# Putting a slice's pending second product directly behind its first product on TensorE, in the first block and a half of a two-layer MLP

## The chip, the cores and the metric

The kernel runs on one core of a Trainium2 chip. The metric is the time of one execution on the device in microseconds (us), the median of several runs. Engines are named as in the profile: PE (TensorE matmul), PEld (its weight load), DVE (VectorE), ACT (ScalarE), POOL (GpSimd), SP (SyncE, which issues the DMAs).

## The reference, cut to what matters

```
a = softmax(scale * x @ state.T)          # per batch and head, 512 x 32
xread = a @ state                         # 512 x 64
a2 = softmax(scale * state @ x.T); sread = a2 @ x
rows = concat([xread, sread]) -> (8 * 544, 512)
h = rows @ w1_in;  g = max(h, 0) + alpha * min(h, 0);  rows = g @ w1_out   # 512 -> 2048 -> 512
h = rows @ w2_in;  g = h - tanh(h);                    out  = g @ w2_out
```

The result is wanted in float32. The matrices are kept as two parts each (a rounded one and what it leaves), and a product is three products of parts.

## The kernel before, in words

The rows are treated in blocks: blocks 0 to 7 are the 512 read rows of a batch, block 8 the 256 state rows. In the first layer a block is worked through in 16 slices of 128 hidden columns (`f` = 0 to 15). A slice has

- a **first product** (`emit_h`, L623) of rows and the slice's columns of `w1_in`, into the PSUM tile `ps_h`: 12 matmuls of 128x128 by 128x512 in block 0, and 6 in blocks 1 to 7, whose weights have been multiplied with the states ahead (`pw`, also kept in `wo` buffers);
- an **activation** in two halves. `act_a`: ACT makes `t` (L629), DVE overwrites `ps_h` (L630). `act_b`: ACT writes the rounded part of `g` (L634), DVE the other part (L635). `g` has two buffers, so `act_b` of slice f overwrites what slice f-2 left;
- a **second product** (`emit_o`, L651): 12 matmuls of 128x512 of `g` and `w1_out`, added up over the slices in four PSUM tiles `acc`. It is done two slices later: slice f's `g` waits in the list `pend`. With a block's (or half block's) last slice, `finish` copies the four `acc` tiles into `y` (ACT L676 takes two, DVE L678 two), and SP stores them.

The order of visits is: slices 0 to 7 of block 0, all 16 of block 1, slices 8 to 15 of block 0, then the other blocks. Below, "slice 0.3" is slice 3 of block 0 and "slice 1.1" slice 1 of block 1.

The program is written in a fixed order. Each engine takes its instructions in that order, waiting on semaphores. Other work is hung into a slice by the timetable `plan`, at five places: `early` (behind the first product, ahead of `act_a`), `gap` and `mid` (behind `act_a`), `late` and `end` (behind `act_b`). The second product of two slices ago stands behind `mid`, ahead of `act_b`:

```
ph = emit_h(blk, n, f)
...            # early
act_a(n, f, ph)
...            # gap, mid
if len(pend) == 2:
    emit_o(*pend.popleft())
pend.append((blk, n, f, act_b(n, f, ph)))
...            # late, end
```

In the stretch of this change what hangs in the timetable is: the attention steps of block 1 (PE transposes `ps_xt` L477 copied by ACT L482, scores `ps_s` L511, softmax on DVE and ACT with the exponential L528, `ps_e` L546 copied by ACT L548, `ps_r` L576 scaled by DVE into `wide` L581 to L586, `ps_w` L601); state transposes (`ps_st` L365, ACT L369 and L376, DVE L377); the projection of weights by states (`ps_p` L414, 3 matmuls in `mid` and 3 in `late`, ACT L421, DVE L422) in slices 0.5, 0.6, 1.0, 1.1, 1.4, 1.5, 1.8 and 1.9; and the conversion of the raw 64-bit weights into parts (ACT L113, L127, L171 or L173; DVE L118, L120, L123; POOL L174, L180 or L183), of which a step hangs in nearly each slice.

All PSUM tiles but `acc` (`ps_h`, `ps_p`, `ps_xt`, `ps_st`, `ps_e`, `ps_s`, `ps_r`, `ps_w` and the conversion's `ps_v`) share four buffers, each handed on when its last reader has been issued; PE then waits for that reader.

Of the kernel before, what the change touches and what calls it, by code (L numbers as in the profile page):

```python
# [35 lines left out]
def attention_and_two_mlps(ctx, tc, x, state, w1_in, w1_out, alpha, w2_in, w2_out, out):  # L36
# [7 lines left out]
    NF = DFF // P  # L44
# [50 lines left out]
    def w_in(f, part):  # L95
        return WI[f // FQ][:, part].rearrange("p c (f m) -> p c f m", f=FQ)[:, :, f % FQ, :]

    def w_out(f, part):
        return WO[f // FQ][:, part, f % FQ, :]
# [251 lines left out]
    def lead(b):  # L351
        return b if b % 2 or b == B - 1 else b - 1
# [260 lines left out]
    def emit_h(blk, n, f):  # L613
        ps = ps_a.tile([P, S], F32, tag="a", name="ps_h")
        if 0 < blk < B:
            col = slice(f % FQ * P, (f % FQ + 1) * P)
            pairs = [([PW[blk, f // FQ, g][i][:, col] for i in range(2)], X[0, blk, g]) for g in range(NG)]
        else:
            w = [WS[f][:, i] if blk else w_in(f, i) for i in range(2)]
            pairs = [([w[i][:, cc, :] for i in range(2)], X[0, blk, cc]) for cc in range(NCC)]  # L620
        for k, (w, xt) in enumerate(pairs):
            for m, (i, j) in enumerate(TERMS):
                nc.tensor.matmul(ps[:, :n], lhsT=w[i], rhs=xt[:, j, :n], start=(k == 0 and m == 0),  # L623
                                 stop=(k == len(pairs) - 1 and m == 2))
        return ps[:, :n]

    def act_a(n, f, ph):
        t = work.tile([P, S], F32, tag="t", name="t")[:, :n]
        nc.scalar.mul(t, ph, slope[:, f:f + 1])  # L629
        nc.vector.scalar_tensor_tensor(ph, ph, sign[:, f:f + 1], t, op0=ALU.mult, op1=ALU.max)  # L630

    def act_b(n, f, ph):
        g = work.tile([P, 2, S], F32R, tag="g", name="g")
        nc.scalar.mul(g[:, 0, :n], ph, sign[:, f:f + 1])  # L634
        nc.vector.scalar_tensor_tensor(g[:, 1, :n], ph, sign[:, f:f + 1], g[:, 0, :n].bitcast(F32),  # L635
                                       op0=ALU.mult, op1=ALU.subtract)
        return g
# [3 lines left out]
    def emit_o(blk, n, f, g):  # L641
        w = [w_out(f, i) for i in range(2)]
        first, last = f == 0, f == NF - 1
        if blk == 0:
            first, last = first or f == NF // 2, last or f == NF // 2 - 1
        if first:
            accs[blk] = [ps_acc.tile([P, S], F32, tag="acc", name="acc") for _ in range(NCC)]
        acc = accs[blk]
        for t in range(NCC):
            for k, (i, j) in enumerate(TERMS):  # L650
                nc.tensor.matmul(acc[t][:, :n], lhsT=w[i][:, t * P:(t + 1) * P], rhs=g[:, j, :n],  # L651
                                 start=(first and k == 0), stop=(last and k == 2))
        if last:
            finish(blk, n, acc)
# [9 lines left out]
    def finish(blk, n, acc):  # L664
        for t, a in enumerate(acc):
            if blk == 0 and half_sum:
                y = half_sum[t]
                nc.vector.tensor_tensor(y, a, y, op=ALU.add)
                stores.append((blk, t, y))
                continue  # L670
            if t < 2:
                y = work.tile([P, S], F32, tag="y", name="y")[:, :n]
            else:
                y = work.tile([P, S], F32, tag="sc" if t == 2 else "at", name="y", bufs=1)[:, :n]
            if t % 2 == 0:
                nc.scalar.copy(y, a[:, :n])  # L676
            else:
                nc.vector.tensor_copy(y, a[:, :n])  # L678
            stores.append((blk, t, y))
# [3 lines left out]
    def store():  # L683
        for blk, t, y in stores:
            nc.sync.dma_start(out=y_dram[blk][t], in_=y)
        stores.clear()
# [407 lines left out]
    with tc.manual_schedule():  # L1094
# [40 lines left out]
        for b in range(2, B):  # L1135
            for g in range(NG):
                i, f = (0, 0) if b == 2 else (b - 2, 6 + 7 * g) if b == lead(b) else (b - 2, 1 + g)
# [78 lines left out]
        pend = deque()  # L1216
        visits = [(0, f) for f in range(NF // 2)] + [(1, f) for f in range(NF)] + [(0, f) for f in range(NF // 2, NF)]
        visits += [(i, f) for i in range(2, len(seq)) for f in range(NF)]
        for i, f in visits:
            blk, n = seq[i]  # L1220
            ph = emit_h(blk, n, f)
            for z in plan.get((i, f, "early"), ()):
                z()
            act_a(n, f, ph)
            for z in plan.get((i, f, "gap"), ()):
                z()
            for z in plan.get((i, f, "mid"), ()):
                z()

            if len(pend) == 2:  # L1230
                emit_o(*pend.popleft())
            pend.append((blk, n, f, act_b(n, f, ph)))
            for z in plan.get((i, f, "late"), ()):
                z()
            for z in plan.get((i, f, "end"), ()):
                z()
            store()
# [125 lines left out]
```

## Time and profile before

| | us |
|---|---|
| time before, median of 3 runs (lowest, highest) | 1465.25 (1464.43, 1468.32) |
| the profiled execution, its own time | 1464.9 |
| its span in the trace | 1463.1 |
| PE busy | 1401.1 (96%) |
| DVE, ACT, POOL busy | 964.2, 731.0, 531.3 |
| first products with `pw`, `wi` and `wo` weights, L623: PE busy | 156.7, 53.3, 20.6 |
| second products, L651: PE busy | 405.6 |

The profile is of one execution, from which all rows below come; its time is 1.8 us over its span. A mean of a group of matmuls is longer than the step from one to the next, because matmuls overlap; the time that twelve take is read from a timeline row. In a timeline row the bracket tells how long the engine was idle before the row and which instruction ended that. PE is the busiest engine, and most of its idle time lies in the first 180 us, where the changed slices are.

### The profile page before, as it was taken

What the parts mean: (1) busy time and instruction counts of PE and PEld (TensorE: products, weight loads), DVE (VectorE), ACT (ScalarE), POOL (GpSimd) and SP (SyncE); (2) the same over time, 40 slices, a digit from 0 to 9 for tenths busy, and PEclk for the clock granted to TensorE, in tenths of its full rate; (3) what the DMA queues carried; (4) which work ended last, traced back from release to release, by engine and by line L of the source; (5) the groups of instructions that cost most, each with busy time, mean ns of one, the idle gap of its engine ahead of it and who ended that gap; (6) DMA issues with size and microseconds to landing.
All of it is one profiled execution on the core that took longest, in us unless ns stands there. A gap on an engine that the chain in (4) does not pass through costs nothing.

```text
span 1463.1 us, 22894 instructions
## 1 busy us (share of the span) xinstructions
PE 1401.1 (96%) x8188; PEld 1189.7 (81%) x8188; DVE 964.2 (66%) x1430; ACT 731.0 (50%) x1322; POOL 531.3 (36%) x414
## 2 busy tenths in 40 slices
PE   5779999999999999999999999999999999999998
PEld 2556777777777777778887888888879999999998
DVE  6888655556667677765345656466347698777774
ACT  4666544445556555655334545455345354444443
POOL 2545410000454455446001212122026576656661
PEclk9999999999999999999999999999999999999999
DMA  5446528885777776769846764553978733444421
GB/s 160 126 140 182 157 77 315 306 277 148 219 196 233 214 249 198 241 212 301 261 129 231 263 244 169 202 194 128 342 279 301 262 107 130 145 138 138 144 80 37
DMA packets 227906, 288.12 MB, mean 197 GB/s; under 512 B 57808, under 2 KB 133584, under 8 KB 226768
## 3 DMA queue, kind: packets, MB, share of 16 engines
q1 hardware_dynamic: 227792, 286.66, 61.0%
q8 instruction: 64, 1.05, 0.3%
q14 instruction: 50, 0.41, 0.1%
HBM read 166.54 MB, written 117.96 MB: 194 GB/s over the span
## 4 chain that ended last, share of the span: by engine, by line
PE 58%; DVE 7%; DMA 7%; ACT 3%; issue 2%; POOL 2%; SPq 1%; ACTq 0%; DVEq 0%; POOLq 0%
PE ps_m L1033 20%; PE ps_m L843 17%; PE acc L651 11%; PE ps_h L623 6%; DMA gt<-g 1%; DMA wp<-wc 1%; DVE ps_h L630 1%; DVE g L635 1%; PE ps_p L414 1%; DMA c_raw<-in_moe_w_in 1%; PE ps_m L917 1%; ACT g L634 1%; DMA g<-ts 1%; DVE c_m L123 1%; DMA c_raw<-in_moe_w_out 1%
## 5 line engine op out<-in xcount | busy, mean ns | idle before, releaser
L651 PE MATMUL acc<-g,wo 128*128 128x512 f32 (+1 forms) x1728 | 405.6, 384 | 3.0 <-ACT g L634 1.1
L651 PEld LDWEIGHTS acc<-g,wo 128*128 128x128 f32 x1728 | 311.2, 190 | 75.2 <-issue 6.5
L1033 PE MATMUL ps_m<-wp,s 128*128 128x256 f32 x2856 | 343.2, 283 | 0.8 <-ACT e L1016 0.8
L1033 PEld LDWEIGHTS ps_m<-wp,s 128*128 128x128 f32 x2856 | 343.0, 192 | 1.1 <-ACT e L1016 1.0
L843 PE MATMUL ps_m<-x,ch 128*128 128x512 f32 x1344 | 306.5, 390 | 3.1 <-ACT c L849 2.4
L843 PEld LDWEIGHTS ps_m<-x,ch 128*128 128x128 f32 x1344 | 251.8, 188 | 57.4 <-ACT c L849 3.7
L978 DVE TENSOR_TENSOR s<-gt,s 128x512 fp32r<-128x512 f32 (+1 forms) x216 | 213.5, 1039 | 45.6 <-ACT s L994 44.6
L635 DVE SCALAR_TENSOR_TENSOR g<-ps_h,sign,g 128x512 fp32r<-128x512 f32 (+1 forms) x144 | 103.6, 720 | 167.0 <-ACT g L634 166.9
L634 ACT ACTIVATE g<-ps_h,sign 128x512 fp32r<-128x512 f32 (+1 forms) x144 | 95.5, 663 | 181.8 <-PE acc L651 130.8
L994 ACT CAST s<-gt 128x512 fp32r<-128x512 f32 (+1 forms) x216 | 120.0, 596 | 82.5 <-PE ps_m L1033 38.4
L623 PE MATMUL ps_h<-x,pw 128*128 128x512 f32 x600 | 156.7, 396 | 3.0 <-DMA pw<-pw 1.6
L630 DVE SCALAR_TENSOR_TENSOR ps_h<-ps_h,sign,t 128x512 f32<-128x512 f32 (+1 forms) x144 | 104.6, 726 | 66.0 <-ACT t L629 65.2
L623 PEld LDWEIGHTS ps_h<-x,pw 128*128 128x128 f32 x600 | 109.7, 188 | 28.6 <-DMA pw<-pw 2.0
L244 POOL TENSOR_TENSOR c_q<-c_m,c_q 128x512 int32<-128x512 int32 x32 | 41.3, 1291 | 241.0 <-DVE c_m L123 222.6
L856 POOL TENSOR_TENSOR t<-c,t 128x512 f32<-128x512 f32 x32 | 44.9, 1402 | 231.0 <-ACT t L853 226.1
L629 ACT ACTIVATE t<-ps_h,slope 128x512 f32<-128x512 f32 (+1 forms) x144 | 95.8, 665 | 54.0 <-PE ps_h L623 53.4
L865 DVE TENSOR_TENSOR c<-ps_m,c 128x512 f32<-128x512 f32 x96 | 65.8, 690 | 83.8 <-PE ps_m L843 71.7
L853 ACT ACTIVATE t<-c 128x512 f32<-128x512 f32 x96 | 60.6, 633 | 85.3 <-DVE c L865 73.8
L271 POOL TENSOR_TENSOR c_o<-c_q,c_o 128x512 fp32r<-128x512 f32 (+1 forms) x48 | 55.8, 1163 | 95.1 <-ACT c_o L269 95.1
L960 POOL TENSOR_TENSOR s<-gt,gt 128x512 f32<-128x512 f32 (+1 forms) x36 | 52.0, 1452 | 87.0 <-DMA gt<-g 86.9
L849 ACT COPY c<-ps_m 128x512 f32<-128x512 f32 x96 | 56.0, 586 | 51.4 <-PE ps_m L843 48.4
L174 POOL TENSOR_TENSOR cq<-cm,cq 128x512 int32<-128x512 int32 x32 | 42.0, 1312 | 105.2 <-DVE cm L123 81.6
(145 smaller groups left out, 1646.8 us busy)
## 6 DMA issues: line engine op xcount, KB each, us to landing
g<-t SPq DMA_DIRECT2D x128, 256.0 KB, 2.3
gt<-g SPq DMA_DIRECT2D x64, 512.0 KB, 5.0
wc<-c_o SPq DMA_DIRECT2D x112, 256.0 KB, 4.0
ch<-wc SPq DMA_DIRECT2D x56, 512.0 KB, 6.8
pw<-pw SPq DMA_DIRECT2D x96, 256.0 KB, 5.4
wp<-wc SPq DMA_DIRECT2D x28, 512.0 KB, 7.0
xr<-in_x SPq DMA_DIRECT2D x64, 128.0 KB, 3.0
raw<-in_moe_w_in SPq DMA_DIRECT2D x16, 512.0 KB, 3.9
```

Source lines behind the costliest of these rows:

```text
L623: nc.tensor.matmul(ps[:, :n], lhsT=w[i], rhs=xt[:, j, :n], start=(k == 0 and m == 0), stop=(k == len(pairs) - 1 and m == 2))
L629: nc.scalar.mul(t, ph, slope[:, f:f + 1])
L630: nc.vector.scalar_tensor_tensor(ph, ph, sign[:, f:f + 1], t, op0=ALU.mult, op1=ALU.max)
L634: nc.scalar.mul(g[:, 0, :n], ph, sign[:, f:f + 1])
L635: nc.vector.scalar_tensor_tensor(g[:, 1, :n], ph, sign[:, f:f + 1], g[:, 0, :n].bitcast(F32), op0=ALU.mult, op1=ALU.subtract)
L651: nc.tensor.matmul(acc[t][:, :n], lhsT=w[i][:, t * P:(t + 1) * P], rhs=g[:, j, :n], start=(first and k == 0), stop=(last and k == 2))
L843: nc.tensor.matmul(b, lhsT=w[p][:, cc], rhs=XT[key, i][cc][:, q], start=(i not in GOES_ON and cc == k == 0), stop=(cc == 1 and k == 2), sk ...
L853: nc.scalar.activation(t, h, AF.Tanh)
L865: nc.vector.tensor_tensor(h, ps[j, i], h, op=ALU.add)
L978: nc.vector.tensor_tensor(made[k - 1][:, 1], src, made[k - 1][:, 0].bitcast(F32), op=ALU.subtract)
L994: nc.scalar.copy(made[k][:, 0], source(blk, i, jj))
L1033: nc.tensor.matmul(dst[:, t * HW:(t + 1) * HW], lhsT=s[:, p, r, t * P:(t + 1) * P], rhs=w[:, q], start=first, stop=(jj == NJ // 2 - 1 and ...
```

## The change

In the first half of block 0 and in block 1 the second product that stands in the list is written directly behind the slice's first product, ahead of `early`. Nothing is added or taken away.

```
--- before.py
+++ after.py
             ph = emit_h(blk, n, f)
+            ahead = len(pend) == 2 and (i == 1 or i == 0 and f < NF // 2)
+            if ahead:
+                emit_o(*pend.popleft())
             for z in plan.get((i, f, "early"), ()):
                 z()
             act_a(n, f, ph)
...
-            if len(pend) == 2:
+            if len(pend) == 2 and not ahead:
                 emit_o(*pend.popleft())
             pend.append((blk, n, f, act_b(n, f, ph)))
```

`pend` holds two entries from slice 0.2 on, so 22 second products move: those written in slices 0.2 to 0.7 and 1.0 to 1.15. `finish` of block 0's first half belongs to the second product written in slice 1.1 and moves with it.

On PE in slice 0.2, the end of the first product and what follows (the difference; `g` is slice 0.0's, `sm` the masked states, `xr` the block's rows; a number behind a name is a running count of buffers):

```order
 L623 MATMUL ps_h<-x_0_3_378,wi_343 128x512 x3
+L651 MATMUL acc<-g,wo_394 128x512 x12
 L365 MATMUL ps_st<-ident,sm 128x128 x2
-L576 MATMUL ps_r<-xr_218,e2t 32x64 x16
-L651 MATMUL acc<-g,wo_394 128x512 x12
-L576 MATMUL ps_r<-xr_218,e2t 32x64 x16
+L576 MATMUL ps_r<-xr_218,e2t 32x64 x32
```

The twelve matmuls of the second product have come past the state transposes and the first `ps_r`.

On PE in slice 1.1, a slice with projections, before:

```order
L623 MATMUL ps_h<-x_1_0_897,wo_904 128x512 x3
L623 MATMUL ps_h<-x_1_1_1103,wo_904 128x512 x3
L414 MATMUL ps_p<-wi_573,snp 128x512 x3
L651 MATMUL acc<-g,wo_756 128x512 x12
L414 MATMUL ps_p<-wi_573,snp 128x512 x3
```

and of the change:

```order
L623 MATMUL ps_h<-x_1_0_909,wo_916 128x512 x3
L623 MATMUL ps_h<-x_1_1_1115,wo_916 128x512 x3
L651 MATMUL acc<-g,wo_756 128x512 x12
L414 MATMUL ps_p<-wi_589,snp 128x512 x6
L623 MATMUL ps_h<-x_1_0_909,wo_916 128x512 x3
```

The two projections, which stood around the second product, now stand together behind it and directly ahead of the next first product.

On ACT in slice 1.1, before (`y<-acc` are the copies of `finish`, `t` and `g` the slice's own activation, `wo` the rounded part of a projection, `cm` a step of the conversion):

```order
L629 ACTIVATE t<-ps_h,slope 128x512
L113 ACTIVATE cm<-raw_1148 128x512
L421 CAST wo_904<-ps_p 128x512
L676 COPY y<-acc 128x512 x2
L634 ACTIVATE g<-ps_h,sign 128x512
```

and of the change:

```order
L676 COPY y<-acc 128x512 x2
L629 ACTIVATE t<-ps_h,slope 128x512
L113 ACTIVATE cm<-raw_1148 128x512
L421 CAST wo_916<-ps_p 128x512
L634 ACTIVATE g<-ps_h,sign 128x512
```

The two copies of `finish` have come ahead of the slice's `t`; on DVE the other two stand ahead of L630 in the same way.

## Rows read from the trace of the kernel before

**Rows 1.** Stretches: us, busy of PE, PEld, DVE, ACT, POOL, PE clock, DMA share, GB/s.

```profile
45.30:110.95 65.65, 50.61 (x323) 36.35 (x324) 52.90 (x95) 38.16 (x74) 30.64 (x24) 0.95 0.43 123
110.95:180.64 69.69, 65.58 (x269) 49.76 (x270) 52.24 (x88) 45.32 (x80) 33.73 (x26) 0.95 0.64 178
180.64:260.00 79.36, 78.61 (x412) 63.24 (x411) 45.50 (x85) 35.30 (x62) 3.83 (x3) 1.00 0.55 190
260.00:300.00 40.00, 37.17 (x170) 28.39 (x172) 23.71 (x43) 18.60 (x36) 0.00 (x0) 1.00 0.96 319
...
76.89:88.64 11.75, 10.22 (x67) 7.55 (x67) 11.13 (x21) 8.10 (x16) 4.98 (x5) 0.85 0.29 94
...
110.95:121.43 10.48, 9.36 (x25) 6.06 (x26) 8.01 (x16) 6.11 (x11) 5.53 (x4) 0.67 0.42 125
```

**Rows 2.** Waits, 45 to 181 us: us in total, times, longest.

```profile
ACT g L634 <- PE acc L651: 25.0, 12, 4.0
...
PE ps_h L623 <- DVE g L635: 4.4, 5, 1.2
```

**Rows 3.** Timeline of slice 0.2: start, us, engine, instruction, idle before it.

```profile
49.73 0.69 PE L365 MATMUL ps_st<-ident,sm 128*128 128x128 f32 x2
50.38 0.70 ACT L629 ACTIVATE t<-ps_h,slope 128x512 f32<-128x512 f32 x1
52.20 3.06 PE L651 MATMUL acc<-g,wo 128*128 128x512 f32 x12
52.95 1.29 POOL L174 TENSOR_TENSOR cq<-cm,cq 128x512 int32<-128x512 int32 x1 [0.26 <-DVE cm L123]
53.30 0.96 DVE L584 TENSOR_SCALAR ri<-par,s 128x2 f32<-128x2 f32 x1
54.37 0.29 DVE L586 TENSOR_TENSOR wide<-ps_r,ri 128x128 f32<-128x128 f32 x1
55.77 3.02 PE L623 MATMUL ps_h<-x,wi 128*128 128x512 f32 x12
57.05 0.23 DVE L584 TENSOR_SCALAR ri<-par,s 128x2 f32<-128x2 f32 x1
```

**Rows 4.** Timeline of slices 0.3 to 0.7, ACT and PE.

```profile
65.54 0.69 ACT L634 ACTIVATE g<-ps_h,sign 128x512 fp32r<-128x512 f32 x1 [3.56 <-PE acc L651]
66.44 3.02 PE L623 MATMUL ps_h<-x,wi 128*128 128x512 f32 x12
76.89 4.60 PE L623 MATMUL ps_h<-x,wi 128*128 128x512 f32 x12 [2.17 <-DVE snp L377]
88.64 3.02 PE L623 MATMUL ps_h<-x,wi 128*128 128x512 f32 x12 [1.20 <-DVE g L635]
98.80 0.69 ACT L634 ACTIVATE g<-ps_h,sign 128x512 fp32r<-128x512 f32 x1 [3.95 <-PE acc L651]
100.33 3.02 PE L623 MATMUL ps_h<-x,wi 128*128 128x512 f32 x12 [0.89 <-DVE g L635]
```

**Rows 5.** Timeline of slice 1.1, PE, ACT and DVE.

```profile
121.43 1.63 PE L623 MATMUL ps_h<-x,wo 128*128 128x512 f32 x6 [0.76 <-DVE g L635]
122.90 0.84 PE L414 MATMUL ps_p<-wi,snp 128*128 128x512 f32 x3
123.10 0.69 ACT L629 ACTIVATE t<-ps_h,slope 128x512 f32<-128x512 f32 x1 [0.84 <-PE ps_h L623]
123.58 2.88 PE L651 MATMUL acc<-g,wo 128*128 128x512 f32 x12
124.23 0.58 ACT L421 CAST wo<-ps_p 128x512 fp32r<-128x512 f32 x1
125.81 0.68 DVE L422 TENSOR_TENSOR wo<-ps_p,wo 128x512 fp32r<-128x512 f32 x1
125.81 0.59 ACT L676 COPY y<-acc 128x512 f32<-128x512 f32 x1 [0.51 <-PE acc L651]
126.98 1.52 PE L623 MATMUL ps_h<-x,wo 128*128 128x512 f32 x6
```

## The prediction

> **What bounds the kernel now.** I read the page first: PE is busy nearly throughout, so time can only be won where PE idles or runs slowly. The view of stretches [rows 1] says where that is. From slice 0.2's first product to block 1's, 45.30 to 110.95 us, PE is busy 50.61 of 65.65 us: 15.0 us idle. To slice 1.12, at 180.64, it is busy 65.58 of 69.69: 4.1 idle. In the next 79.36 us it idles 0.75 us. In the two changed stretches the granted clock is 0.95, elsewhere here 1.00; by slices the loss sits in few of them (0.85 in 0.5, 0.67 in 1.0). So some 19 us of idle time, and a few more of half clock, are all that this change can touch.
>
> Then the view of waits [rows 2]. The wait that the change aims at is there: ACT's first write of `g` waits for the second product of two slices ago 12 times, 25.0 us in all, up to 4.0. It has to, since that product reads the buffer that `g` overwrites. But PE, which is the bound, waits for what follows from it (DVE's half of `g`) only 5 times, 4.4 us. What PE mostly waits for in these slices is the rest of a ring: PE side work, ACT, DVE, a PSUM buffer, the next first product. That ring is asked slice by slice below.
>
> **The change part by part.** No instruction is added or removed on any engine, and SP's and POOL's order is the same; 22 second products move. In seven of them (1.2, 1.3, 1.6, 1.7, 1.12 to 1.14) PE has nothing between first and second product, so nothing moves. In the other 15, three things happen. ACT's write of `g` no longer waits for the second product. All PE side work of `early`, `gap` and `mid` starts one second product later, 2.9 us. And `finish` of block 0's half comes ahead of slice 1.1's activation. I follow how late the next first product is against before.
>
> *Slice 0.2, 1.5 us late.* The state transpose stands in `early`, and ACT's copies of it stand ahead of `t`. Now it comes 2.9 us later: `t` starts at 50.38 + 2.9 = 53.3 [rows 3]. From the start of `t` to the end of `wide` it took 54.66 - 50.38 = 4.3 us; DVE had first to finish a conversion step, which is done by then, so I take 4.0. The next first product needs the PSUM buffer that `wide` frees: 57.3 instead of 55.77. Before, PE was in the second product (52.20 to 55.26) while that chain ran, and it is idle during it now.
>
> In this chain DVE's tiny `ri` took 0.96 us at 53.30 and 0.23 at 57.05. The first stands behind POOL's add, which ends at 52.95 + 1.29 = 54.24, and `ri` ends at 54.26 [rows 3]. [...] The 4.0 above keeps it, by the row.
>
> *Slices 0.3 and 0.4, -0.5 and +0.35.* In 0.3 the transposes `ps_xt` come later and push `t` in the same way, but the wait of 3.56 us ahead of `g` [rows 4] is gone, and what stood behind the second product (`ps_s`, next first product) no longer does: 10.2 us instead of 55.77 to 66.44, 10.67. DVE's work behind it stays about 1.35 late. In 0.4 ACT waits for the softmax anyway while PE does the second product: DVE's 1.35 becomes the next first product's.
>
> *Slices 0.5 and 0.6, -0.65 and -1.0.* These are where the change does what it can. The first products of 0.6 and 0.7 waited 1.20 and 0.89 us for DVE's half of `g` [rows 4]. That of 0.6 now gets the buffer of the first `ps_p`, whose reader stands one DVE operation ahead (0.65). In 0.6 `t` is pushed by 3.0 but the wait of 3.95 ahead of `g` goes (1.0). Lateness at 0.7's first product: -0.3.
>
> *Slices 0.7 and 1.0, +0.85 and 0.* The second projection of 0.6 needs the buffer that DVE's reading of the first one frees. That now follows behind the pushed `t`, so DVE's next work, the softmax, starts some 0.5 late, and it runs without a gap to the first product of 1.0: +0.85 against -0.3. In 1.0 the second product and a projection change places in the half clock [rows 1]: the same 15 matmuls, the same time.
>
> *Slice 1.1, +2.1.* The second copy of `finish` cannot start before the third `acc` tile is done, 125.81 - 123.58 = 2.23 us after the second product starts [rows 5]. That product now starts 1.5 us after the first, so the copy starts at 3.7 and `t`, now behind it, at 4.25 us, instead of 123.10 - 121.43 = 1.67. DVE's reading of the projection ended 126.49 - 123.10 = 3.4 us after the start of `t`; now at 7.65. The next first product needs that buffer: 7.7 us after this one instead of 126.98 - 121.43 = 5.55. Before, the second product covered this.
>
> *Projection slices 1.4, 1.5, 1.8, 1.9, and 1.10, 1.11: +0.5 together.* Now both projections stand directly ahead of the next first product, which needs the first one's buffer: 0.84 on PE, 0.58 on ACT, 0.68 on DVE and the hand-overs are 2.2 us, of which the second projection covers 1.5 [rows 5]. That is 0.7 idle a slice, about what PE idled in them before for `g` (part of the 4.4). I take +0.2, -0.4, 0 and +0.4, and +0.3 for the copy of `ps_xt` ahead of `t` in 1.10 and 1.11.
>
> *Sum:* 1.5 - 0.5 + 0.35 - 0.65 - 1.0 + 0.85 + 2.1 + 0.5 = +3.2 us at slice 1.12. From there PE is busy 99% up to 260 us, and the order is as before, so the lateness is carried to the end. Only between 260 and 300, with 2.8 us of PE idle [rows 1], could some be absorbed; the transfers there follow work that is late too, and I take nothing off. Against the profiled execution's own 1464.9 (its span is 1463.1) this gives 1468.1; that execution lies 0.35 under the median, so beside the median it is 1468.45. I predict 1468.3, 0.2% more, within the 0.3% (4.4 us) that a measurement of this kernel can tell from no change.
>
> Bounds of what no row shows. The gains cannot be more than the 4.4 us of PE waiting for `g`, unless the ring as a whole turns faster: then at most the 15.0 us. The losses are 0 to 1.5 in 0.2 (0 if PE's next product finds another buffer), 0 to 2.6 in 1.1 (the push of `t`), and 0 to 0.7 in each of the other eight, 5.6.
>
> **The rivals.** *Slower: half clock behind a longer gap.* [...] My 0.2 leaves PE with little but small transposes for nearly 4 us ahead of 0.3's first product. If the clock drops there, 0.3 costs 1.6 more, and all later steps hang on it: 3.2 + 1.6 = 4.8, 1469.9; once more in 1.1, where PE would idle 1.9 us, 1471.5. It decides from 1.2 us on, since that passes 4.4. [...] Against: the gap of 1.20 ahead of 0.6 was followed by 3.02. [...]
>
> *Faster: the 25.0 us of ACT's waiting were the ring.* Freed, ACT and DVE would run ahead with conversions and softmax, and a third of the 15.0 us would close: 1465 - 5 = 1460. For it: the wait of 3.95 us in 0.6 ends 1.5 us before the next first product [rows 4]. Against: only 4.4 us of them reach PE, and in slices with an `early` step ACT now waits for the same 2.9 us one operation sooner, ahead of `t`.
>
> *Nothing: the losses are covered.* The lateness is given back by the idle time up to 300 us, or 0.2 and 1.1 find other buffers: 0 to +1, 1465.5. For it: PE idles 2.8 us there. Against: its cause is late as well.
>
> That the second products do not move can be left out: the order of instructions shows it.
>
> **How the numbers follow.** Forecast, +1 to +4.4 us: 0.45. Covered: 0.12. Slower rival, with what of my losses exceeds their size: 0.33. Faster rival: 0.10. So slower by over 0.3% 0.33, within 0.3% 0.57, faster 0.10. The range takes in the slower rival with both drops and some error on top, 1473.5, and goes down to 1462, leaving most of the faster one out; the forecast's own range is 1466 to 1469.7.
>
> **What would show it.** In the profile after: ACT's `g` waits for `acc` only in the seven unmoved slices and in block 0's second half, under 10 us; ACT's `t` or the copies ahead of it wait instead. The first product of 0.3 comes near 57.3, of 0.7 near 100.0, of 1.2 near 129.7, of 1.12 near 184. The clock of 0.3 (1.00 or not) tells the slower rival. I am wrong if the first product of 1.0 comes much before 110.95, if 1.1 lasts under 6.5 us, or if what is lost by 1.12 is not there at 420 us.

## The result: 0.5% slower

The changed kernel takes 1472.91 us (median of 5 runs, 1471.34 to 1476.58) against 1465.53 for the kernel before in the same comparison (5 runs, 1464.43 to 1468.32). The ratio is 1.0051, 95% interval 1.0034 to 1.0069: 7.4 us slower, more than the 0.3% that can be told from no change. That lies inside the range of the prediction, but its forecast, a loss too small to be told from no change, did not come. What came is the slower rival. The profiled execution took 1476.58 us (span 1474.8), the slowest of the five.

The lengths of the slices, from one first product to the next, in the two profiled executions:

| slice | before | after | difference | forecast |
|---|---|---|---|---|
| 0.2 | 10.47 | 11.81 | +1.34 | +1.5 |
| 0.3 | 10.67 | 12.97 | +2.30 | -0.5 |
| 0.4 | 10.45 | 11.85 | +1.40 | +0.35 |
| 0.5 | 11.75 | 11.64 | -0.11 | -0.65 |
| 0.6 | 11.69 | 10.67 | -1.02 | -1.0 |
| 0.7 | 10.62 | 11.57 | +0.95 | +0.85 |
| 1.0 | 10.48 | 9.85 | -0.63 | 0 |
| 1.1 | 5.55 | 7.76 | +2.21 | +2.1 |
| 1.2 | 4.08 | 5.83 | +1.75 | 0 |
| 1.3 to 1.11 | 49.58 | 50.48 | +0.90 | +0.5 |

In sum 9.1 us at slice 1.12 where 3.2 were forecast. Four terms are right within 0.2; 0.3, 0.4 and 1.2 miss by 2.8, 1.05 and 1.75, all upward.

### The profile page after: what moved, and what is told of

It is laid out like the page before. It is cut to its first block, busy times and chain, and to the rows that moved or that the text cites. A ratio compares the mean times of both kernels' runs of the same rounds, so it can differ in the third digit from the quotient of the medians.

```text
span 1474.8 us, 22891 instructions
## 1 busy us (share of the span) xinstructions
PE 1408.8 (96%) x8188; PEld 1196.4 (81%) x8188; DVE 965.6 (65%) x1430; ACT 730.2 (50%) x1322; POOL 534.3 (36%) x414
## 3 DMA queue, kind: packets, MB, share of 16 engines
q8 instruction: 64, 1.05, 0.3%
## 4 chain that ended last, share of the span: by engine, by line
PE 55%; DMA 8%; DVE 7%; ACT 3%; issue 2%; POOL 2%; SPq 1%; ACTq 0%; DVEq 0%; POOLq 0%
PE ps_m L1033 20%; PE ps_m L843 17%; PE acc L651 10%; PE ps_h L623 5%; DMA gt<-g 1%; PE ps_m L917 1%; DVE ps_h L630 1%; DMA wp<-wc 1%; DVE g L635 1%; DMA c_raw<-in_moe_w_in 1%; ACT g L634 1%; PE ps_p L414 1%; DMA pw<-pw 1%; DVE c_m L123 1%; DVE c_m L120 1%
## 5 line engine op out<-in xcount | busy, mean ns | idle before, releaser
L651 PEld LDWEIGHTS acc<-g,wo 128*128 128x128 f32 x1728 | 314.8, 191 | 74.6 <-issue 5.0
L630 DVE SCALAR_TENSOR_TENSOR ps_h<-ps_h,sign,t 128x512 f32<-128x512 f32 (+1 forms) x144 | 104.5, 726 | 77.4 <-ACT t L629 76.9
```

## The profile after

The stretches, of the same slices as in [rows 1] (us, busy of PE, PEld, DVE, ACT and POOL, PE clock, DMA share, GB/s):

```profile
44.57:115.08 70.51, 55.01 (x323) 40.86 (x324) 53.31 (x95) 37.93 (x74) 30.59 (x24) 0.85 0.39 114
115.08:189.00 73.92, 67.18 (x270) 50.97 (x270) 52.62 (x89) 45.11 (x81) 33.74 (x26) 0.94 0.61 168
189.00:268.36 79.36, 78.61 (x412) 63.31 (x413) 45.30 (x85) 34.81 (x61) 3.83 (x3) 1.00 0.55 190
268.36:308.36 40.00, 37.22 (x174) 28.41 (x176) 23.69 (x43) 17.93 (x36) 0.00 (x0) 1.00 0.96 320
```

The first stretch is 4.86 us longer, yet PE idles 15.50 us in it where it idled 15.04: the same matmuls are just busy for 4.4 us more, and the clock is 0.85 instead of 0.95. In the third stretch PE's busy time is the same to 0.01 us as before: nothing is given back.

The wait that the change aimed at, 45 to 190 us (us in all, times, longest):

```profile
DVE ps_h L630 <- ACT t L629: 16.3, 11, 5.3
...
ACT g L634 <- PE acc L651: 5.4, 3, 3.1
...
PE ps_h L623 <- DVE wo L422: 4.0, 4, 2.0
...
PE ps_h L623 <- DVE g L635: 1.0, 3, 0.3
```

Against [rows 2], ACT's waits for the second product fall from 25.0 us to 5.4, and PE's for DVE's half of `g` from 4.4 to 1.0. So the change does what it says, but other waits grow: DVE waits 16.3 us for a later `t`, where it waited 7.4 before, and PE 4.0 us for DVE's reading of a projection (`wo`).

PE in 0.2, and the first products of 0.3 to 0.5 (start, us, instruction, idle before it and what ended it):

```profile
49.02 2.90 PE L651 MATMUL acc<-g,wo 128*128 128x512 f32 x12
51.76 0.38 PE L365 MATMUL ps_st<-ident,sm 128*128 128x128 f32 x2
52.88 0.65 PE L576 MATMUL ps_r<-xr,e2t 128*32 128x64 f32 x32 [0.74 <-DVE snp L377]
54.62 0.65 PE L576 MATMUL ps_r<-xr,e2t 128*32 128x64 f32 x32 [1.08 <-ACT snp L376]
56.38 5.49 PE L623 MATMUL ps_h<-x,wi 128*128 128x512 f32 x12 [1.10 <-DVE wide L586]
...
68.08 0.33 PE L601 MATMUL ps_w<-ident,wide 128*128 128x128 f32 x1 [1.64 <-DVE cm L123]
...
69.35 4.61 PE L623 MATMUL ps_h<-x,wi 128*128 128x512 f32 x12
...
81.20 5.43 PE L623 MATMUL ps_h<-x,wi 128*128 128x512 f32 x12 [2.90 <-DVE snp L377]
```

Three stretches of the same execution, the small steps of 0.2, all of 0.3 and all of 0.4 (columns as above):

```profile
51.76:56.38 4.62, 1.69 (x68) 1.16 (x66) 3.31 (x9) 4.31 (x11) 1.99 (x3) 0.93 0.34 110
56.38:69.35 12.97, 11.09 (x38) 7.91 (x38) 7.08 (x15) 4.87 (x9) 4.44 (x4) 0.76 0.20 64
69.35:81.20 11.85, 8.21 (x33) 6.33 (x31) 9.21 (x17) 5.94 (x14) 5.74 (x6) 0.79 0.35 102
```

In [rows 3] the second product stood between the small steps and covered the chain to `wide`. Now PE is busy 1.69 of 4.62 us ahead of 0.3, and then 12 matmuls that took 3.02 us [rows 3] take 5.49: the granted clock is 0.50 through them, where it was 1.00 through the same twelve before. 0.50 is called the lower level below, 1.00 the upper. The lower one comes again in 0.4 (first product 4.61 instead of 3.02, its mean clock 0.63) after 1.64 us of idle and a few small matmuls, and lasts longer in 0.5 (5.43 instead of 4.60, mean clock 0.52 instead of 0.63) after 2.90.

In 0.2 the rest is as forecast: POOL's add still stands ahead of DVE's tiny `ri`, which ends with it at 55.9 (0.96 us in [rows 3], 0.81 here):

```profile
54.62 1.28 POOL L174 TENSOR_TENSOR cq<-cm,cq 128x512 int32<-128x512 int32 x1 [2.63 <-ACT snp L376]
...
54.74 0.14 DVE L581 TENSOR_SCALAR s<-s 128x1 f32<-128x1 f32 x1
...
55.12 0.81 DVE L584 TENSOR_SCALAR ri<-par,s 128x2 f32<-128x2 f32 x1
```

The prediction's 4.0 us for this chain kept the 0.96 by the row, and the long `ri` came again. DVE's `s` ran its 0.14 us inside the same add, while `ri` ended only with it. In the kernel before, the nine `ri` that start outside a POOL step took 0.23 us each; the seven that start inside one took up to 1.17, and each ended 0.02 to 0.04 us behind that step. Why `ri` was held and `s` was not, no run here shows.

Slices 1.1 and 1.2 of after, ACT, DVE and PE:

```profile
124.93 1.65 PE L623 MATMUL ps_h<-x,wo 128*128 128x512 f32 x6 [0.33 <-DVE g L635]
126.42 2.90 PE L651 MATMUL acc<-g,wo 128*128 128x512 f32 x12
128.68 0.59 ACT L676 COPY y<-acc 128x512 f32<-128x512 f32 x1 [0.77 <-PE acc L651]
129.16 0.69 ACT L629 ACTIVATE t<-ps_h,slope 128x512 f32<-128x512 f32 x1
131.96 0.68 DVE L422 TENSOR_TENSOR wo<-ps_p,wo 128x512 fp32r<-128x512 f32 x1
132.69 1.66 PE L623 MATMUL ps_h<-x,wo 128*128 128x512 f32 x6 [2.00 <-DVE wo L422]
134.18 4.50 PE L651 MATMUL acc<-g,wo 128*128 128x512 f32 x12
```

`t` starts 4.23 us after the first product (forecast 4.25; 1.67 in [rows 5]), DVE's reading ends 7.71 us after it (7.65), the next first product comes at 7.76 (7.7). Behind the 2.00 us of idle, the second product of 1.2 takes 4.50 us, at a mean clock of 0.62, where others take 2.88.

## The experiments

**Theory.** Two losses add up: late steps, as in the prediction's sum (some 3.5 us), and TensorE's lower clock level where the moved second product leaves PE idle (0.3, 0.4, 1.2; some 5.5 us). **Rivals:** the late steps alone, the level being chance; the level being there but covered by other waits; only the copies ahead of `t`, or only TensorE's order, costing.

Each kernel was compared with the kernel before on the same chip; "time" is the ratio less one, times 1466 us, with its interval. "Late" is the time from 0.2's first product to that of 1.0, 1.1 or 1.12 in its profiled execution, less that in the profile of [rows 1 to 5].

| kernel | late at 1.0 | at 1.1 | at 1.12 | time |
|---|---|---|---|---|
| before_again | 1.5 | 2.1 | 2.2 | 0 (itself) |
| changed | 4.9 | 4.2 | 9.1 | +7.4 (5.0 to 10.1) |
| only_half0 | 4.0 | 3.3 | 3.6 | +1.9 (0.4 to 3.5) |
| only_block1 | 1.3 | 1.7 | 4.7 | +4.0 (2.3 to 5.6) |
| busy_02_03 | 1.2 | 0.5 | 5.0 | +4.3 (2.5 to 5.9) |
| after_busy | 0.7 | -0.9 | 3.7 | +10.8 (8.4 to 13.3) |
| before_busy | 1.5 | 1.4 | 1.4 | 0.0 (-2.1 to 1.9) |
| not_02 | 0.5 | -0.1 | 2.9 | +1.2 (0.0 to 2.5) |
| not_11 | 3.9 | 3.4 | 4.0 | +1.6 (0.3 to 3.1) |
| t_first | 0.7 | 0.4 | 3.5 | 0.0 (-1.8 to 1.6) |
| proj_later | 3.9 | 3.6 | 6.7 | +6.0 (4.0 to 7.9) |
| only_05_06 | 0.9 | 1.3 | 1.7 | -0.7 (-2.1 to 0.6) |
| best | -1.3 | -1.1 | -1.3 | -1.9 (-3.7 to 0.0) |

**A control.** The kernel before, unchanged, profiled once more.

> The kernel before once more, unchanged, for a second profile of it: three kernels whose 0.3 is that of before had its second product at the lower clock level (4.3 us instead of 3.0), the one profiled execution of before had not. If that is how the kernel before mostly runs, 0.3 lasts 12.0 us here instead of 10.67, and the changed kernel's lateness of 9.1 us overstates the difference by 1.3; if not, 10.67.

0.3 lasts 12.27 us:

```profile
61.47 0.33 PE L601 MATMUL ps_w<-ident,wide 128*128 128x128 f32 x1 [1.82 <-DVE cm L123]
61.55 4.58 PE L651 MATMUL acc<-g,wo 128*128 128x512 f32 x12
```

Its second product falls to the lower level behind 1.82 us of idle, as in only_block1, only_05_06, before_busy and best, whose 0.3 has the old order too. So the profile that the prediction was worked out from was the exception among six. If the lateness of this control stands for the kernel before, 2.2 us are to be taken off the column "at 1.12" to compare with times. Then the changed kernel is 6.9 late (measured 7.4), and every kernel but after_busy agrees with its time within 1.7 us. That is an estimate from one execution for each kernel.

**One half of the change each.**

```
-ahead = len(pend) == 2 and (i == 1 or i == 0 and f < NF // 2)
+ahead = len(pend) == 2 and i == 0 and f < NF // 2        # only_half0
+ahead = len(pend) == 2 and i == 1                        # only_block1
```

> The second products stand ahead only in block 0's first half; block 1 has its old order. Theory (late steps plus TensorE's half clock): the first products of 0.3, 0.4 and 0.5 run at the lower clock level as in the changed kernel (5.5, 4.6, 5.4 us instead of 3.0, 3.0, 4.6), slice 1.1 lasts 5.55 us again, so +4.2 us remain at 1.1 and to the end: 1469.7 us (1468.5 to 1470.5). Rival (only the order's waits cost, and the clock dropped in that one execution by chance): the terms of block 0 alone, +0.55: 1466 us, with all of 0.3 and 0.4 at 1.00.

> The second products stand ahead only in block 1; block 0 has its old order. Theory: 1.1 lasts 7.7 us instead of 5.55, the idle time ahead of 1.2 brings the lower clock level there (+1.6), and the projection slices add up to 0.9, so +3 to +4.9: 1469.5 us (1468.5 to 1470.5). Rival (the loss in 1.1 is covered, block 0 costs all): 1465.5 to 1466.5.

In only_half0 the level falls in 0.3 and 0.4 as in the changed kernel (first products of 5.49 and 4.33 us); not_11 and proj_later, with the same order in 0.2, have 5.49 in 0.3 as well, so it isn't chance. 0.5's first product takes 4.28 us instead of the expected 5.4. The time is lower than the theory's, by about what the control takes off. In only_block1 slice 1.1 lasts 7.78 us and the projection slices add 0.6, but the level of 1.2 stays up, behind the same gap:

```profile
129.61 1.66 PE L623 MATMUL ps_h<-x,wo 128*128 128x512 f32 x6 [2.00 <-DVE wo L422]
131.11 2.88 PE L651 MATMUL acc<-g,wo 128*128 128x512 f32 x12
```

So the expected fall in 1.2 did not come, and the time, +4.0, is in the expected range without it. The two halves together are +5.9, and the changed kernel +7.4: they add up within the intervals.

**TensorE kept busy.** Matmuls that add zero (`zero` is a small tile, cleared at the start) to an open accumulator stand where PE idled. The edit of busy_02_03, cut to its calls:

```
+def busy(k):
+    for _ in range(k):
+        nc.tensor.matmul(accs[0][0], lhsT=w_out(0, 0)[:, :P], rhs=zero[:, :1].to_broadcast([P, S]), start=False, stop=False)
-at(0, 2, "mid", a.s5)
-at(0, 2, "late", c.s5)
-at(0, 3, "mid", a.s6, c.s6)
+at(0, 2, "mid", partial(busy, 3), a.s5)
+at(0, 2, "late", partial(busy, 4), c.s5)
+at(0, 3, "mid", a.s6, partial(busy, 6), c.s6)
+busy({(0, 3): 4}.get((i, f), 0))     # ahead of the first product; after_busy has more ahead of 0.5 and 1.0
```

> The changed kernel with only the 17 matmuls of zero in 0.2 and 0.3 (3 and 4 around the ps_r of 0.2, 4 ahead of 0.3's first product, 6 between the ps_w of 0.3); nothing is added ahead of 0.5 and 1.0. Theory: 0.3's and 0.4's first products take 3.0 us, at 0.5's first product the kernel is 1 us late instead of 5.0, from there on as the changed kernel (4 to 6 us late at 1.12), and the whole is 4 us slower than before instead of 7.4. Rival (the clock of these slices isn't what costs; what is won there is lost later, as with the 36 matmuls): 4 to 6 us late at 1.12, but 7 to 11 us in all.

The small steps of 0.2, then 0.3 and 0.4 in busy_02_03:

```profile
51.55:56.16 4.61, 4.49 (x78) 2.98 (x76) 3.29 (x9) 4.30 (x11) 1.95 (x3) 1.00 0.34 95
...
56.16:66.29 10.13, 9.56 (x45) 6.83 (x45) 7.10 (x15) 4.89 (x9) 4.47 (x4) 1.00 0.29 90
66.29:77.50 11.21, 6.61 (x33) 5.12 (x31) 9.22 (x17) 5.83 (x15) 5.72 (x6) 0.91 0.37 106
```

This is the run that decides. The same stretch of 4.6 us, the same other engines, PE busy 4.49 instead of 1.69 us: 0.3 is at 1.00 and lasts 10.13 (the prediction's 10.2 without a fall), 0.4's first product takes 3.01. At 1.1 it is 0.5 us late instead of 4.2, so the level there costs 3.75 us: 2.85 in 0.3, 0.6 in 0.4, and 0.3 in what follows. The time follows, 4.3 over before where 4 was expected; its interval (2.5 to 5.9) still overlaps the changed kernel's (5.0 to 10.1), so the 3.75 rests on the slices. 1.2 falls to the lower level here too (its second product 4.50). In the changed kernel the level fell though no gap in the small steps ahead of 0.3 was over 1.10 us, with tiny matmuls between them. The added matmuls both close the gaps and raise PE's busy time, so the runs don't tell which of the two kept the level.

> The changed kernel, with 36 more matmuls that add zero to an open accumulator, in the places of block 0 where TensorE idled: 3 and 4 around the two ps_r of 0.2, 4 ahead of 0.3's first product, 6 between the two ps_w of 0.3, 11 ahead of 0.5's first product, 8 and 10 around ps_r ahead of 1.0's. By the duration of a matmul of this shape (0.24 us) they take 11 us, nearly all of it in time that TensorE idled. Theory (it is the idle time that brings the lower level): 0.3, 0.4, 0.5 and 1.0 run at the upper level; back come 2.9 + 1.6 + 2.4 + up to 3.5 us, less some 1 us that the added work stands in the way: 1464.5 us (1462.5 to 1467). Rival 1 (the lower level is there, but the ring would make TensorE wait anyway): first products 3.0 us, but longer waits behind them; 1470 to 1473. Rival 2 (the level does not hang on this idle time): first products as long as in the changed kernel; 1473 to 1475.

(It has 46 added matmuls, 3 + 4 + 4 + 6 + 11 + 8 + 10, not the 36 of the text above, and 17 of them are those of busy_02_03.) By its slices 0.3 to 0.5 are the theory's own case, with first products of 3.0 us. At 1.0 it is 0.7 late, where the prediction's terms without a fall give 1.5 - 0.5 + 0.35 - 0.65 - 1.0 + 0.85 = 0.55, but that agreement is luck. 0.2's own first product took 3.02 us here, behind 2.48 us of idle that the edit leaves alone, and 4.33 to 4.62 in the 13 other profiles. 0.6's took 4.59 instead of 3.02: 0.5's second projection waited 1.38 us for a buffer, and the level fell behind that. The two cancel. And its time is 10.8 us over before, against 1.5 by its lateness (3.7 less 2.2). In its profile 1.4 us of the missing come between 471 and 489 us (on the clock of the kernel before) and 4.3 between 695 and 702, where ACT waits for a transfer of another step:

```profile
702.61 0.40 ACT L270 CAST c_o<-c_q 128x256 fp32r<-128x256 f32 x1 [4.87 <-DMA wc<-c_o]
```

Before, the same wait is 2.45 us. Why it is longer here stays open. With 17 matmuls instead of 46 it did not come, but the profiled execution of best, without any, also loses 7.3 us behind 1.12.

```
+busy({(0, 5): 8, (1, 0): 10}.get((i, f), 0))    # before_busy: ahead of the first product
+busy({(0, 7): 4}.get((i, f), 0))                # and behind 0.7's second product
```

> The kernel before, with 22 such matmuls of zero: 8 ahead of 0.5's first product (2.17 us idle there), 4 and 10 around ps_r ahead of 1.0's (1.23 and 2.52 idle). Theory: 0.5's first product takes 3.0 us instead of 4.6, and 1.0 loses its half clock (first product 1.5 instead of 3.2, the projection 0.8 instead of 1.65, the second product 2.9 instead of 3.9): up to -5 us, 1461 us (1460 to 1463). Rival (what is won there is waited for behind it): 1465 to 1466; a level that does not hang on the idle time: 1465.5 to 1466.5 with the same durations.

0.5's first product does take 3.02 us instead of 4.60, yet 0.5 lasts 11.73 instead of 11.75: the projection behind it now waits 1.91 us for a PSUM buffer that DVE has to free.

```profile
77.17 3.02 PE L628 MATMUL ps_h<-x,wi 128*128 128x512 f32 x12 [0.43 <-DVE snp L378]
80.12 0.65 PE L577 MATMUL ps_r<-xr,e2t 128*32 128x64 f32 x32
82.68 0.96 PE L415 MATMUL ps_p<-wi,snp 128*128 128x512 f32 x3 [1.91 <-DVE cm L124]
```

The fall in 0.5 costs nothing. In 1.0 the level still fell (its second product takes 4.50 us). The first rival, then, and it limits the theory: a fall costs only where PE is what the slice waits for, as in 0.3, 0.4 and 1.2. Other runs show the bound for 0.5. In the changed order it lasts 11.04 us with a first product of 3.01 (after_busy), 11.06 with 4.61 (only_05_06) and 11.64 with 5.43 (the changed kernel): what goes beyond some 4.6 us costs.

**Single slices undone.**

```
+ahead = len(pend) == 2 and (i == 1 or i == 0 and 2 < f < NF // 2)             # not_02
+ahead = len(pend) == 2 and (i == 1 and f != 1 or i == 0 and f < NF // 2)      # not_11
```

> As the changed kernel, but slice 0.2 keeps its old order. Theory (the small PE steps of 0.2, which the second product no longer covers, bring the lower clock level of 0.3 and 0.4): 0.2 lasts 10.5 us, 0.3's and 0.4's first products take 3.0 us each instead of 5.5 and 4.6; then at 1.0 the kernel is 1.0 to 0 us ahead of the kernel before; block 1 costs as before, +3.4 to 5.2 at 1.12. In all +3.5 us, 3.9 less than the changed kernel. Rival (the level falls in 0.3 for another reason): first products as in the changed kernel, +1.3 us less at 1.0, in all +6.

0.3's first product takes 3.01 us and 0.3 lasts 10.09, so it is 0.2's order that brings the fall of 0.3. PE in not_02:

```profile
54.56 3.01 PE L623 MATMUL ps_h<-x,wi 128*128 128x512 f32 x12
...
63.38 0.33 PE L601 MATMUL ps_w<-ident,wide 128*128 128x128 f32 x1 [1.64 <-DVE cm L123]
...
64.65 4.58 PE L623 MATMUL ps_h<-x,wi 128*128 128x512 f32 x12
```

0.4's takes 4.58: that fall comes from 0.3's own gap of 1.64 us, and the expectation for 0.4 missed. Where that gap is filled (busy_02_03) or gone (0.19 us in t_first), 0.4's takes 3.01. At 1.0 it is 0.5 late instead of up to 1 ahead, at 1.12 2.9. The time, +1.2, is under the +3.5 expected, by the 2.2 of the control.

> As the changed kernel, but slice 1.1 keeps its old order, so block 0's two copies stand behind the activation again. Theory: 1.1 lasts 5.6 us instead of 7.76 and 1.2 4.1 instead of 5.83 (no idle time of 2 us ahead of it, so no lower clock level): 4.0 us less, 5 us late at 1.12 instead of 9.1; in all +3.5 us. Rival (the push comes back in the next projection): 1.1 5.6, but the sum over 1.1 to 1.5 within 1 us of the changed kernel's; +6.5.

1.1 lasts 5.58, 1.2 4.08, and nothing comes back in 1.3 to 1.5. That gives back 3.9 us, as said. At 1.12 it is 4.0 late where 5 was said, because it is only 3.9 late at 1.0 instead of 4.9, with shorter falls in 0.4 and 0.5 (4.28 and 4.33). The time, 1.6, is under the 3.5 expected, by the 2.2 of the control.

**The activation first.** TensorE's order stays as changed. The edit, cut to its calls:

```
-    emit_o(*pend.popleft())
+    emit_o(*pend.popleft(), defer=True)     # finish deferred
+    act_a(n, f, ph)
+    while ended: finish(*ended.pop())
 for z in plan.get((i, f, "early"), ()): z()
-act_a(n, f, ph)
+if not ahead: act_a(n, f, ph)
```

> TensorE's order is that of the changed kernel, but in every slice with the second product ahead ACT's t (and DVE's step on it) stand ahead of the copies of early and ahead of finish. Theory (two costs: copies ahead of t, and TensorE's own side work behind the second product): 1.1 lasts 6.6 us instead of 7.76, by the projection that is copied from PSUM 0.6 + 0.7 us after it ends at 5.2 us, and the lower level of 1.2 goes (-1.7); 0.2 0.3 us less, and 0.3 still has the lower level; in all +4 us instead of +7.4. Rival (only the copies ahead of t cost): 0.2 10.5, 1.1 5.6, no lower level in 0.3: 0 to +1 us. Rival (only TensorE's order costs): 1.1 7.5 to 7.8 as in the changed kernel, +7 us.

0.2 loses 0.29 instead of 1.34, so most of its loss was the order on ACT and DVE. Of these 1.05 us, 0.47 is `ri`, which takes 0.34 us here and again ends with POOL's add. 0.3's first product takes 4.61 us, a shorter fall, and 0.4's 3.01. But 1.1 still lasts 7.08 (6.6 expected): of its 2.2 us only 0.7 are the copies ahead of `t`:

```profile
122.65 2.88 PE L653 MATMUL acc<-g,wo 128*128 128x512 f32 x12
125.37 1.52 PE L414 MATMUL ps_p<-wi,snp 128*128 128x512 f32 x6
125.57 0.69 DVE L682 COPY y<-acc 128x512 f32<-128x512 f32 x1 [0.65 <-PE acc L653]
126.18 0.68 DVE L118 TENSOR_SCALAR ps_v<-cm 128x512 f32<-128x512 f32 x1
126.25 0.59 ACT L421 CAST wo<-ps_p 128x512 fp32r<-128x512 f32 x1 [0.21 <-PE ps_p L414]
126.89 0.70 DVE L120 TENSOR_SCALAR ps_v<-ps_v 128x512 int32<-128x512 int32 x1
127.50 0.68 DVE L422 TENSOR_TENSOR wo<-ps_p,wo 128x512 fp32r<-128x512 f32 x1
128.24 0.96 PE L623 MATMUL ps_h<-x,wo 128*128 128x512 f32 x3 [1.35 <-DVE wo L422]
```

`t` starts 1.69 us after the first product here, and still the next one waits for DVE's reading of a projection. Two chains end near that reading. PE begins the projections only behind the second product, so ACT's part is ready at 126.84. DVE comes later: its second copy of `finish` waits 0.65 us for `acc`, and from there it works without a gap up to the reading at 127.50. So it is still `finish`, now on DVE, that ends last; the place of the projections alone would have held the reading to 126.84. That is read from the rows; no run separates the two. With 1.35 us of idle 1.2 stays at the upper level (clock 1.00 over the slice). In time the kernel is level with before, 4 us better than the theory. That is the time of the first rival (only the copies ahead of `t` cost), but the slices are not: 1.1 lasts 7.08 where it says 5.6, and the level falls in 0.3.

**The term of 0.7.**

```
-at(i, f, "late", partial(project_one, b, q, g, 1))
+at(i, f, "end" if (i, f) == (0, 6) else "late", partial(project_one, b, q, g, 1))
```

> The changed kernel, but in 0.6 the copy and reading of the second projection stand behind the start of the softmax on ACT and DVE. Tests the term of 0.7 (+0.85 forecast, +0.95 measured: DVE idles 0.94 us for that copy, and then works without a gap up to the step that frees 1.0's PSUM buffer). Theory: the softmax's transpose starts at 103.4 instead of 104.94 us, the copy costs 0.8 of that back, and 1.0's first product comes 0.7 us earlier against 0.7's: 0.7 lasts 10.9 instead of 11.57; in all 0.7 less than the changed kernel, +6.7. Rival (1.0 is set by ACT or a transfer): 11.4 to 11.6.

0.7 lasts 10.61 us instead of 11.57 (10.9 expected). DVE's softmax starts at 103.96, 0.30 us ahead of 0.7's first product, instead of 1.43 behind it:

```profile
103.30 0.74 DVE L635 SCALAR_TENSOR_TENSOR g<-ps_h,sign,g 128x512 fp32r<-128x512 f32 x1
103.96 0.71 DVE L517 STREAM_TRANSPOSE sc<-ps_s 128x512 f32<-128x512 f32 x1
...
107.37 0.69 DVE L422 TENSOR_TENSOR wi<-ps_p,wi 128x512 fp32r<-128x512 f32 x1
```

So that term was DVE's chain, as the prediction said. The time, +6.0, is as expected.

**Toward a better kernel.**

```
+ahead = len(pend) == 2 and i == 0 and f in (5, 6)     # only_05_06; best with the two edits above as well
```

> Only the second products of 0.5 and 0.6 stand ahead, where the change won by its slices (-0.1 and -1.0 us; 0.5 lost in it 0.8 to a longer half clock). Theory: 0.5 lasts 11.1 (-0.65), 0.6 10.7 (-1.0), 0.7 10.9 (+0.3 since DVE's reading of 0.6's projection comes later): 1.3 us ahead at 1.0, and at the end 1.3 us less than the kernel before, inside what can be told from no change. Rival 1 (half of 1.0 is longer at the lower level, since TensorE idles longer ahead of it): -1.3 + 1.3, nothing left. Rival 2 (the freed ring runs on): 3 us or more ahead at 1.0.

0.5 lasts 11.06 and 0.6 11.04, so 1.3 are won by 0.7. But 0.7 lasts 11.64 where 10.9 was expected and gives 1.0 of it back: no change that can be told.

> What the runs point to: only the second products of 0.5 and 0.6 stand ahead, with t ahead of the copies of early there, and the second projection of 0.6 read behind the start of the softmax. Theory: 0.5 lasts 11.0, 0.6 10.4, 0.7 11.3: 1.5 to 2 us ahead of the kernel before at 1.0's first product, counted from 0.5's; in all 1466 where the kernel before has 1467.8, inside what can be told from no change. Rival (1.0 hangs on DVE's softmax whatever is won in 0.5 and 0.6): -1.5 at 0.7, but not more than -0.3 at 1.0; no change.

0.5 lasts 10.42, 0.6 10.13 and 0.7 10.66: counted from 0.5's first product 2.85 us are won up to 1.0, more than the 1.5 to 2 expected, and it is 1.3 ahead up to 283 us (its profiled execution, the slowest of its 12, loses more than that later). The ratio is 0.9987 (0.9975 to 1.0000): the sign and size expected, but it can't be told from no change. It is the only one of the eleven whose interval does not reach above the kernel before.

## Why the prediction was right in its range and wrong in its forecast

*What bounds the kernel.* It bounded what can be won rightly, but the loss came from half clock that was not there before (0.50 through 0.3's first product, 1.00 before): in the first stretch PE idles as long as before and is busy 4.4 us longer. And the 25.0 us of ACT's waiting were not the ring: 19.6 of them went, and PE's waiting for `g` fell by 3.4 us, but 0.5 and 0.6 won just 1.1. The faster rival is out.

*0.2, +1.5.* Right, +1.34, with its reason, the copies ahead of `t`: t_first gives back 1.05 of it.

*0.3 and 0.4, -0.5 and +0.35.* Here the forecast failed. The terms themselves hold while the clock stays: 0.3 lasts 10.13 in busy_02_03 (10.2 forecast). What failed is the step that PE's small steps in 0.2 are harmless to the clock in the forecast's own case. I had priced one fall in 0.3 at 1.6 us and given it 0.33. The 1.6 was an estimate, 4.60 less 3.02 of two other slices' first products [rows 4]; 0.3's own lost 2.47 (5.49). The fall cost 3.75 with the one in 0.4, which comes from 0.3's own gap (not_02). The argument against it was a gap of 1.20 us ahead of 0.6 that was followed by 3.02. The gap ahead of 0.3 was no longer, 1.10 us, but it ended a stretch in which PE had been busy 1.69 of 4.62 us.

*0.5, 0.6, 0.7.* -0.11, -1.02 and +0.95 for -0.65, -1.0 and +0.85. 0.5 lost its gain to a longer fall: with one of the old length, in only_05_06, it is -0.69. The mechanism of 0.7 is shown by proj_later.

*1.0 and 1.1.* 0 and +2.1 came as -0.63 and +2.21. For 1.0 that is about what two profiles of one kernel differ by: it lasts 10.48 us in the first profile of the kernel before and 11.00 in the control. The size of 1.1 is right, and not_11 shows that it is this slice's order. The reason was put too narrowly: I put it on `finish` ahead of `t`, but with `t` first 1.5 of the 2.2 us stay, because DVE's copies of `finish` still stand ahead of its reading, with the place of the projections close behind as a second reason.

*1.2.* The rival had a second fall behind 1.1's gap of 1.9 us: it came (2.00 us, 1.75 lost) in the changed kernel, after_busy and busy_02_03, not in only_block1, not_02 and proj_later behind a gap of 2.00 or 2.01. What decides between them is open.

*Projection slices, +0.5.* +0.9: under the bounds, the sum of many small terms mis-sized by 0.4.

*The sum and the base.* Without the falls of 0.3, 0.4 and 1.2 the terms came to 0.5 + 2.2 + 0.9 = 3.6 for 3.2 forecast. The falls add 3.75 + 1.75, 9.1 in all. The base was wrong the other way: the one profiled execution of the kernel before lacked a fall that five others of the same 0.3 have, worth some 2 us. So about 6.9 of the 9.1 is what the median can show, as an estimate. That the lateness is carried on was right: 8.9 to 9.1 up to 310 us, and 9.4 at 416. Between there and 760 us this execution loses 2.9 us more, and it lies 3.7 us above the median of its five. The profiles of best and after_busy lose 3.8 and 6.6 us in the same stretch; what brings that stays open.

## What to carry to other kernels

A large block of matmuls between small dependent steps did two things at once here: it covered their chain, and it kept TensorE's clock up. Before moving such a block, look at all that PE is left to do in its place, and not only at the longest gap: the clock fell behind 1.69 us of work in 4.62 with no gap over 1.10, and did not fall with 4.49 in 4.61. Price a fall of the clock at its full length where PE is what the slice waits for. Profile the kernel before a second time when falls of the clock are at stake, since one execution can lack what the others have.

## What the runs showed of the hardware that was not expected

- Matmuls that add only zero held the clock at 1.00: 11 of them in a stretch of 4.6 us (PE busy 4.49 instead of 1.69), with six more in 0.3, won 3.75 us.
- The same gap of 2.00 to 2.01 us ahead of the same instruction was followed by the lower level in some kernels' executions (the second product 4.50 us) and not in others (2.88). The kernel before itself had the fall in 0.3 in one profile (second product 4.58, behind 1.82 us of idle) and not in the other (2.99, behind 1.81).
- A fall that comes while another engine holds the slice cost nothing here: 1.6 us less of first product in 0.5 changed the slice by 0.02.
